# Scores and masks of unit 15 eight slots later in the fourth group's first step

## The chip, the cores and the metric

The kernel runs on one core of a Trainium2 chip. The core has a matrix engine (TensorE, PE in the profile; its weight loads stand apart as PEld), VectorE (DVE), ScalarE (ACT), GpSimd (POOL) and SyncE (SP), which issues most of the DMAs. The metric is the device time of one execution in microseconds, as the median of several runs.

## What is computed

Two stages follow each other: a linear attention with decay, block by block, and a bilinear feed-forward layer on its output.

```python
for b in range(nb):
    qb, kb, vb = (q[:, :, sl], k[:, :, sl], v[:, :, sl])
    intra = np.einsum('bhic,bhjc->bhij', qb, kb) * Dmask[None]
    intra = np.einsum('bhij,bhjd->bhid', intra, vb)
    inter = np.einsum('bhid,bhde->bhie', qb * lam_pow[None], kv_state)
    out[:, :, sl] = intra + inter
    kb_dec = kb * rev_pow[None]
    kv_state = lam_block * kv_state + np.einsum('bhsd,bhse->bhde', kb_dec, vb)
...
a = x @ w_a
b = x @ w_b
return a * b @ w_out
```

There are 4 batches, 8 heads, 768 positions and a head size of 64; x has 3072 rows of 512, and the hidden size is 1536.

## The kernel before

**Units and groups.** The 3072 rows are cut into 24 *units* of 128 positions (six for each batch), and the units into seven groups of 4, 2, 4, 4, 4, 4 and 2. While the feed-forward layer of one group runs, the attention of later units is fitted in between. The fourth group (group 3 in the code) holds units 10 to 13; during it the attention of units 14 to 17 is computed, which are the rows of the fifth group.

**What one unit's attention needs.** Its q and k are loaded by SP. POOL multiplies them by powers of the decay into one bf16 tile qk (line 276), then issues the load of v (line 298). SP transposes the tile by DMA into qkT (line 310). PE computes the unit's scores, eight matmuls into two banks of PSUM named kq (line 343, `scores`), and DVE multiplies each bank by a triangle of ones, giving two masked tiles m (line 360, `mask`). Together these last two are the piece "S" of the plan. Later a piece "O2" or "Q" adds up the outputs of two units from qkT, m, v and the running state. Piece "P" is POOL's scaling and all that hangs on it.

**The feed-forward layer of a full group** (`ffn_seven`) replaces eight block products by seven, with sums of blocks. Six *rounds* (0 to 5) cover the hidden size, two tiles of 128 at a time. Each round has seven products, called 1, 5, 2, 6, 3, 7 and 4 in the order in which they start, of four matmuls each (line 564), into accumulators m_q (1, 6, 7, 4), m_r (5, 3) and m_p (2). Between them ScalarE copies accumulators into SBUF (line 579) and DVE adds: c11 (line 598; in round 0 of this group on POOL, line 601), c12 (line 609), c22 (line 615), and the second half of the result ab (line 618). POOL makes the first half of ab (line 611) from c11 and c12. The tile of c12 has two buffers, so the c12 of one round waits for POOL's ab of two rounds before. The rounds overlap:

```python
for off, m in ((0, 1), (2, 5), (3, 2), (4, 6), (6, 3), (8, 7), (12, 4)):
    at[7 * i + off] = (i, m)
```

Then `out_seven` multiplies ab by the output weights in the same manner, beginning with o_q (line 675), which reads the POOL half of rounds 0, 2 and 4; DVE sums blocks of ab for it (lines 708 to 714) and the next group's rows (xs, lines 542 to 545).

**What sets the order.** Each engine runs its instructions in the order in which the program issues them. The table `PLAN` says for each group at which slot which piece is issued. In the rounds, slot 0 comes behind the first product of round 0, and slot 7 behind product 6 of round 3; slots 11 and later lie behind the rounds and in the output stage. At slot 17 of the group before, a piece "G" makes POOL wait for the sums xs of the next group, and the pieces "P" of units 15 and 16 stand behind it; those of units 17, 18 and 19 stand at slots 1, 4 and 7 of the fourth group. Seven banks of PSUM go round: a new accumulator takes the one that was longest out of use.

Of the kernel before, what the change touches and what calls it, by code (L numbers as in the profile page):

```python
# [22 lines left out]
def _bc(ap, dims):  # L23
# [33 lines left out]
        (6, "V", 8), (6, "P", 11), (7, "S", 9), (12, "O2", (8, 9))],  # L57
    2: [(0, "TO", 1), (0, "TO", 2), (0, "GT", None), (1, "P", 12), (4, "P", 13), (7, "P", 14), (10, "S", 10), (11, "S", 11),
        (17, "G", None), (17, "P", 15), (17, "P", 16)],
    3: [(0, "S", 15), (1, "P", 17), (4, "P", 18), (7, "P", 19), (17, "G", None), (17, "P", 20)],  # L60
    4: [(1, "P", 21), (4, "P", 22), (7, "P", 23)],
    5: [(11, "V", 22), (13, "O2", (22, 23))],
}
# [996 lines left out]
```

## Time and profile before

| what | us |
|---|---|
| median of 3 runs | 225.63 (225.57 to 226.48) |
| profiled execution | 225.45 |
| its span in the trace | 223.2 |
| PE busy | 211.4 (95%) |
| DVE busy | 175.2 (78%) |
| POOL busy | 126.5 (57%) |
| ACT busy | 109.4 (49%) |
| mean granted clock of PE | 0.985 of full speed |

The span runs from the first to the last instruction of the trace; the rest of the execution's time lies around it. A row of a timeline gives the start from the span's beginning, the length, the engine, the line, the operation with output and inputs, how many instructions were merged, and in brackets how long the engine stood idle before it and what ended that. A row of the windows gives the stretch, its length, then the busy time of PE, PEld, DVE, ACT and POOL with counts, the granted clock, the DMA share and the rate. The list of waits has the total, the number and the longest.

### The profile page before, as it was taken

The numbers are of one execution on the slowest core, as the hardware profiler recorded it, in microseconds if no ns is written. First come the engines' busy times: TensorE is split into PE (matmuls) and PEld (weight loads), VectorE is DVE, ScalarE is ACT, GpSimd is POOL, SyncE is SP. The second block draws the span as 40 slices with busy tenths as digits, with TensorE's granted clock in tenths as the row PEclk, the third lists the DMA queues.
The fourth block names the chain that finished last, engine by engine and source line by source line (L and its number), as shares of the span: only waits on it lengthen the run. The fifth ranks groups of instructions, "written<-read, shape, count | busy, mean of one in ns | idle before, by whom it ended". The sixth has DMA issues, their size and how long they took to land.

```text
span 223.2 us, 5802 instructions
## 1 busy us (share of the span) xinstructions
PE 211.4 (95%) x2339; PEld 163.8 (73%) x2347; DVE 175.2 (78%) x320; ACT 109.4 (49%) x199; POOL 126.5 (57%) x144
## 2 busy tenths in 40 slices
PE   7799999999999999999199999999999999999994
PEld 2476444557985888877078888788887888889973
DVE  0992999867888987999058899978899887996860
ACT  3586233358842755454055545275637366443522
POOL 5879659955676599505559940479930065310230
PEclk9999999999999999999679999999999999999999
DMA  4999999999799999991999993199950310001302
GB/s 132 291 181 187 202 228 213 226 222 155 147 162 167 142 151 217 266 149 51 188 245 150 181 152 54 49 194 176 105 49 3 139 52 0 3 0 54 138 3 94
DMA packets 84654, 30.78 MB, mean 138 GB/s; under 512 B 71956, under 2 KB 81044, under 8 KB 84628
## 3 DMA queue, kind: packets, MB, share of 16 engines
q1 hardware_dynamic: 51636, 19.86, 45.4%
q0 software_dynamic: 32704, 10.49, 41.6%
q8 instruction: 18, 0.29, 0.6%
q10 hardware_dynamic: 288, 0.07, 0.1%
q14 instruction: 8, 0.07, 0.1%
HBM read 28.32 MB, written 6.29 MB: 155 GB/s over the span
## 4 chain that ended last, share of the span: by engine, by line
PE 84%; issue 5%; DMA 5%; POOL 1%; SPq 1%; DVE 1%; ACT 0%; POOLq 0%
PE m_q L564 24%; PE m_r L564 12%; PE op L801 9%; PE o_q L675 7%; PE m_p L564 6%; PE b_ps L487 5%; PE a_ps L487 5%; PE o_ps L379 4%; PE o_r L675 4%; DMA k<-in_k_dram 3%; DMA qkT<-qk 2%; PE kq L343 2%; PE o_p L675 2%; SPq L229 1%; PE tps L321 1%
## 5 line engine op out<-in xcount | busy, mean ns | idle before, releaser
L564 PEld LDWEIGHTS <-tw 128*128 128x128 bf16 x576 | 49.3, 98 | 5.8 <-issue 0.2
L611 POOL TENSOR_TENSOR ab<-c,c 128x512 bf16<-128x512 bf16 x30 | 34.8, 1168 | 29.9 <-DVE c L609 29.6
L564 PE MATMUL m_q<-xs,tw 128*128 128x256 bf16 (+1 forms) x288 | 36.6, 257 | 0.0
L360 DVE TENSOR_TENSOR m<-kq,lotri 128x512 bf16<-128x512 f32 x47 | 29.5, 681 | 7.7 <-PE kq L343 7.7
L564 PEld LDWEIGHTS <-wa_sb 128*128 128x128 bf16 x288 | 25.0, 99 | 2.9
L579 ACT COPY s<-m_q 128x512 f32<-128x512 f32 x30 | 17.7, 590 | 16.8 <-PE m_q L564 15.7
L618 DVE TENSOR_TENSOR ab<-c,m_q 128x512 bf16<-128x512 f32 x30 | 20.6, 685 | 6.7 <-PE m_q L564 4.5
L609 DVE TENSOR_TENSOR c<-u,m_r 128x512 f32<-128x512 f32 x30 | 20.4, 681 | 5.2 <-ACT u L579 2.9
L579 ACT COPY s<-m_r 128x512 f32<-128x512 f32 x30 | 17.7, 590 | 13.3 <-PE m_r L564 13.3
L298 POOL DMA_DIRECT2D vb<-in_v_dram x24 | 22.3, 933 | 1.4 <-DMA wo_sb<-in_moe_w_out_dram 1.2
L801 PE MATMUL op<-wo_sb,ab 128*128 128x512 bf16 (+2 forms) x114 | 22.1, 335 | 0.4 <-issue 0.2
L601 POOL TENSOR_TENSOR c<-s 128x512 bf16<-128x512 f32 x7 | 9.1, 1295 | 21.3 <-ACT s L579 21.3
L615 DVE TENSOR_TENSOR c<-s,m_q 128x512 f32<-128x512 f32 x30 | 20.6, 686 | 0.6
L579 ACT COPY u<-m_q 128x512 f32<-128x512 f32 x30 | 17.8, 593 | 6.6 <-PE m_q L564 6.3
L675 PEld LDWEIGHTS <-sm 128*128 128x128 bf16 x192 | 17.5, 98 | 3.6 <-DVE sm L714 0.4
L598 DVE TENSOR_TENSOR c<-s,m_p 128x512 bf16<-128x512 f32 x23 | 15.8, 687 | 5.2 <-PE m_p L564 5.0
L276 POOL TENSOR_TENSOR qk<-qf,lp_q 128x512 bf16<-128x512 f32 x18 | 18.8, 1044 | 1.3 <-DMA qf<-in_q_dram 1.3
L564 PE MATMUL m_p<-xT,wa_sb 128*128 128x256 bf16 (+1 forms) x144 | 18.5, 259 | 0.0
L564 PE MATMUL m_r<-xs,tw 128*128 128x256 bf16 (+1 forms) x144 | 18.5, 259 | 0.0
L564 PE MATMUL m_r<-xs,wb_sb 128*128 128x256 bf16 (+1 forms) x144 | 18.4, 258 | 0.0
L402 ACT CAST xT<-o_ps 128x512 bf16<-128x512 f32 x22 | 11.9, 589 | 12.7 <-PE o_ps L379 12.4
L564 PE MATMUL m_q<-xT,tw 128*128 128x256 bf16 (+1 forms) x144 | 18.1, 255 | 0.0
(119 smaller groups left out, 376.0 us busy)
## 6 DMA issues: line engine op xcount, KB each, us to landing
out_dram<-o_two SPq DMA_DIRECT2D x8, 512.0 KB, 3.5
qf<-in_q_dram SPq DMA_DIRECT2D x14, 256.0 KB, 5.3
kf<-in_k_dram SPq DMA_DIRECT2D x14, 256.0 KB, 5.5
vb<-in_v_dram POOLq DMA_DIRECT2D x24, 128.0 KB, 5.5
wa_sb<-in_moe_w_a_dram POOLq DMA_DIRECT2D x6, 256.0 KB, 6.2
wb_sb<-in_moe_w_b_dram POOLq DMA_DIRECT2D x6, 256.0 KB, 7.7
wo_sb<-in_moe_w_out_dram POOLq DMA_DIRECT2D x6, 256.0 KB, 8.1
out_dram<-o_kept SPq DMA_DIRECT2D x6, 256.0 KB, 4.5
```

The source lines that it names most:

```text
L276: eng_of(eng).tensor_mul(dst.rearrange("p (c b) d -> p b c d", b=2), x[:].rearrange("p (b c) d -> p b c d", b=2), lp.rearrange("p (b c) o ...
L298: nc.gpsimd.dma_start(out=vb, in_=vr[b, nb])
L360: nc.vector.tensor_mul(m, kq[i], lotri_bc)
L487: nc.tensor.matmul(ps[:, lo:hi], lhsT=w_sb[:, s, f * 128:(f + 1) * 128], rhs=xT[:, s, lo:hi], start=(s == 0), stop=(s == KS - 1), skip_gro ...
L564: nc.tensor.matmul(ps[:, f, :], lhsT=w(k, f), rhs=x[:, k, :], start=(first and f == 0 and k == 0), stop=True, skip_group_check=True)
L579: nc.scalar.copy(t, ps)
L609: nc.vector.tensor_add(c12, d["u2"], d["r"])
L611: nc.gpsimd.tensor_mul(ab[:, nf * i:nf * i + nf, 0:h], d["c11"], c12)
L615: nc.vector.tensor_add(d["c22"], d["s5"], d["q"])
L618: nc.vector.tensor_mul(ab[:, nf * i:nf * i + nf, h:2 * h], d["c22"], d["q"])
L675: nc.tensor.matmul(ps[:, t, :], lhsT=x(j, c)[:, t * BLK:(t + 1) * BLK], rhs=w(j)[:, c, :], start=(first and t == 0 and j == js[0] and c == ...
L801: nc.tensor.matmul(op[:, lo:hi], lhsT=ab[:, f, t * 128:(t + 1) * 128], rhs=wo_sb[:, f, lo:hi], start=(f == 0), stop=(f == FC - 1))
```

## The change

One entry of the plan moves: the piece "S" of unit 15 goes from slot 0 of the fourth group to slot 7, ahead of the piece "P" of unit 19.

```diff
-    3: [(0, "S", 15), (1, "P", 17), (4, "P", 18), (7, "P", 19), (17, "G", None), (17, "P", 20)],
+    3: [(1, "P", 17), (4, "P", 18), (7, "S", 15), (7, "P", 19), (17, "G", None), (17, "P", 20)],
```

On PE, at the start of the fourth group, the program before has the last matmul of product 1 and then the scores of unit 15 (a row is a line of the code, the instruction and its operands with the tiles' numbers; in brackets stand the counters that it waits for, DMAHW being those of SP's DMAs):

```order
L564 LDWEIGHTS wa_sb_96
L564 MATMUL m_q_1957<-xT_1331,wa_sb_96 128x256
L343 LDWEIGHTS qkT_1908 [waits DMAHW1_49]
L343 MATMUL kq0_1964<-qkT_1908 128x128 [waits Activation_49]
L343 LDWEIGHTS qkT_1908
L343 MATMUL kq1_1965<-qkT_1908 128x128 [waits Activation_49]
```

With the change the same place reads so:

```order
L564 LDWEIGHTS wa_sb_96
L564 MATMUL m_q_1957<-xT_1331,wa_sb_96 128x256
L564 LDWEIGHTS tw_495
L564 MATMUL m_r_1964<-xs_1861,tw_495 128x256 [waits Activation_49]
L564 LDWEIGHTS tw_495
```

Product 5 of round 0 (m_r) now follows product 1 directly, and the weight load that waits for the transposing DMA is gone from here. On PE behind product 6 of round 3 (m_q_2104), the change has:

```order
L564 LDWEIGHTS tw_574
L564 MATMUL m_q_2104<-xs_1861,tw_574 128x256
L343 LDWEIGHTS qkT_1908 [waits DMAHW1_49]
L343 MATMUL kq0_2137<-qkT_1908 128x128 [waits DVE_49]
L343 LDWEIGHTS qkT_1908
L343 MATMUL kq1_2138<-qkT_1908 128x128 [waits DVE_49]
```

The wait for the DMA moves with the scores; behind the eight score matmuls comes product 4 of round 2. On DVE, at the group's start, the program before has the masks of unit 14, those of unit 15, and the first sums of round 0 and 1:

```order
L360 TENSOR_TENSOR m_1937<-kq_1927,lotri 128x512
L360 TENSOR_TENSOR m_1939<-kq_1928,lotri 128x512
L360 TENSOR_TENSOR m_1974<-kq_1964,lotri 128x512
L360 TENSOR_TENSOR m_1976<-kq_1965,lotri 128x512
L609 TENSOR_TENSOR c_2014<-u_1997,m_r 128x512
```

With the change the masks of unit 15 (m_2147 and m_2149) stand in rounds 2 and 3, behind c22 of round 2 and c11 of round 3:

```order
L615 TENSOR_TENSOR c_2115<-s_2077,m_q 128x512
L598 TENSOR_TENSOR c_2129<-s_2109,m_p 128x512
L360 TENSOR_TENSOR m_2147<-kq_2137,lotri 128x512
L360 TENSOR_TENSOR m_2149<-kq_2138,lotri 128x512
L618 TENSOR_TENSOR ab<-c_2115,m_q 128x2x256
L609 TENSOR_TENSOR c_2171<-u_2135,m_r 128x512
L615 TENSOR_TENSOR c_2185<-s_2122,m_q 128x512
```

So on DVE they come ahead of the second half of ab of round 2 and of c12 and c22 of round 3. ScalarE, POOL and SP have the same instructions in the same order as before.

## The prediction

> **What bounds the kernel now.** I read the page first, then the list of waits, then the chain that ended last around the longest wait, then the timeline and the windows of that stage. The page says which engine to watch:
>
> ```profile
> span 223.2 us, 5802 instructions
> ## 1 busy us (share of the span) xinstructions
> PE 211.4 (95%) x2339; PEld 163.8 (73%) x2347; DVE 175.2 (78%) x320; ACT 109.4 (49%) x199; POOL 126.5 (57%) x144
> ```
>
> TensorE (PE) is busy nearly all the time, so what is to be gained is where it stands still or runs slowly. In the list of waits, PE's longest is this one:
>
> ```profile
> PE kq L343 <- DMA qkT<-qk: 5.3, 1, 5.3
> ```
>
> It happens once. The timeline of PE puts it behind the first product of the fourth group (round 0, product 1), and the third row shows where that group's rounds end and its first output product begins:
>
> ```profile
> 105.08 0.60 PE L564 MATMUL m_q<-xT,wa_sb 128*128 128x256 bf16 x4
> 110.95 0.61 PE L343 MATMUL kq<-qkT 64*128 64x128 bf16 x8 [5.27 <-DMA qkT<-qk]
> ...
> 130.78 1.47 PE L675 MATMUL o_q<-wo_sb,ab 128*128 128x256 bf16 x12
> ```
>
> The chain that ended last shows what the eight score matmuls waited for, and what followed:
>
> ```profile
> 105.39 5.52 DMA qkT<-qk
> 110.91 0.04 issue
> 110.95 0.61 PE kq L343 x6
> 111.56 0.97 PE m_r L564 x4
> 112.53 0.85 PE m_p L564 x4
> 113.38 0.85 PE m_q L564 x4
> 114.23 0.77 PE m_r L564 x4
> 115.00 0.87 PE m_q L564 x8
> ```
>
> GpSimd (POOL) had only just scaled unit 15; its transposing DMA started at 105.39 and landed at 110.91. The four products after the wait are slow as well: 0.97, 0.85, 0.85 and 0.77 us where eight matmuls take 0.87, so 0.435 for four. That is 3.44 - 4 x 0.435 = 1.70 us of slow clock. The windows agree; the first is the fourth group's rounds, the second those of the fifth, which does the same products without scores among them, and the third lies just behind the wait (the column before the last two is the granted clock):
>
> ```profile
> 105.08:130.78 25.70, 20.43 (x178) 17.36 (x176) 15.32 (x24) 11.62 (x20) 19.80 (x20) 0.87 1.36 190
> 144.32:162.62 18.30, 18.30 (x170) 16.25 (x168) 15.06 (x24) 11.33 (x20) 16.72 (x17) 1.00 1.18 165
> 111.00:115.00 4.00, 4.00 (x26) 2.85 (x27) 1.29 (x2) 1.76 (x3) 0.91 (x1) 0.53 1.55 224
> ```
>
> So the fourth group's rounds take 7.40 us longer than the fifth's. 5.27 is the wait, 1.70 the slow clock, and the remaining 0.43 about what eight score matmuls take.
>
> **The change, part by part.** No instruction is added or removed. The unit's eight score matmuls go behind product 6 of round 3, their two masks on VectorE (DVE) before that round's next instruction, and the banks of PSUM are dealt out in another order within the group. POOL and SyncE (SP) keep their order, so no DMA is moved.
>
> *Removed at the old place.* Product 5 of round 0 follows product 1 at once. Had PE nothing else to wait for, the group would take 18.30 us as the fifth does, plus the scores. The scores have a price inside a group in the third one:
>
> ```profile
> 87.61 0.60 PE L564 MATMUL m_q<-xs,tw 128*128 128x256 bf16 x4
> 88.14 0.40 PE L343 MATMUL kq<-qkT 64*128 64x128 bf16 x8
> 88.47 0.61 PE L564 MATMUL m_r<-xs,tw 128*128 128x256 bf16 x4
> ```
>
> From 87.61 to 88.47 are 0.86 us, less 0.44 for the four matmuls of m_q: 0.42. PE alone would reach o_q at 105.08 + 18.30 + 0.42 = 123.80, a gain of 6.98. The scores themselves come at about 115.74 in the new place (product 4 of round 3, placed at 118.79 below, less the seven products of a round, 7 x 0.435), 4.8 us after the transposed tile has landed.
>
> *What POOL allows.* POOL does not wait for PE at the group's start; it is busy with unit 16:
>
> ```profile
> 108.26 0.94 POOL L298 DMA_DIRECT2D vb<-in_v_dram  x1
> 114.09 1.26 POOL L601 TENSOR_TENSOR c<-s 128x512 bf16<-128x512 f32 x1 [4.89 <-ACT s L579]
> ...
> 118.27 2.30 POOL L611 TENSOR_TENSOR ab<-c,c 128x512 bf16<-128x512 bf16 x2
> ...
> 124.60 1.04 POOL L276 TENSOR_TENSOR qk<-kf,lp_k 128x512 bf16<-128x512 f32 x1
> ...
> 127.54 2.29 POOL L611 TENSOR_TENSOR ab<-c,c 128x512 bf16<-128x512 bf16 x2
> 131.25 1.17 POOL L611 TENSOR_TENSOR ab<-c,c 128x512 bf16<-128x512 bf16 x1 [1.42 <-DVE c L609]
> ```
>
> Its sum c11 of round 0 now has its operands early, but POOL comes free only at 108.26 + 0.94 = 109.20 instead of 114.09. From there to 129.83 (the end of the ab product of round 4) it ran without a gap, so the whole row moves by 4.89 us and no more: the ab products of rounds 0 and 1 to 113.38, that of round 4 ends at 129.83 - 4.89 = 124.94. PE needs it for the fifth of the twelve matmuls of o_q, 0.44 after o_q begins. Before, that was 131.22, and POOL was done 1.39 ahead. Now PE would ask at 124.24 and POOL answers at 124.94: **POOL ends last**.
>
> *What DVE costs.* Two delays fall on DVE, both read against the fifth group, whose times I move by 144.32 - 105.08 = 39.24:
>
> ```profile
> 153.16 0.68 DVE L609 TENSOR_TENSOR c<-u,m_r 128x512 f32<-128x512 f32 x1
> ...
> 156.92 0.69 DVE L615 TENSOR_TENSOR c<-s,m_q 128x512 f32<-128x512 f32 x1
> ...
> 158.03 0.60 PE L564 MATMUL m_q<-xT,tw 128*128 128x256 bf16 x4
> ```
>
> The sum c12 of round 2 (153.16, so 113.92 here) writes a buffer, one of two, which the ab product of round 0 reads until about 113.38 + 1.15 = 114.53: it starts some 0.65 late. Queued behind it are c22 of round 2, c11 of round 3, the two masks, and then ab, c12 and c22 of round 3, each some 0.6 after the one ahead (the two masks before were busy 1.29 together, the only DVE work from 111 to 115). Counted from 114.6 that puts c22 of round 3 at 118.8, ending at 119.5. Product 4 of round 3 (158.03, so 118.79, plus 0.42 for the scores: 119.21) waits for it: about 0.35 us. DVE is busy 15.06 of 18.30 us in the fifth group, so it catches up. So PE reaches o_q at 123.80 + 0.35 = 124.15 and its fifth matmul at 124.59. That is still before POOL's 124.94, which with some 0.04 to pass the signal (110.91 to 110.95 at the old wait) makes 125.0.
>
> *Masks at the old place* cost nothing before, as DVE stood idle there, and their removal gives nothing. ScalarE's copies only follow PE. The first rounds now take their banks of PSUM from the same predecessors as those of the fifth group, where PE is busy 18.30 of 18.30 us; the scores take theirs from sums of rounds 1 and 2, which are done by then.
>
> *The new short wait and the clock.* By the rows a wait of 0.4 us costs between no slow clock and a share of what the long one cost, 1.70 x 0.4 / 5.27 = 0.13; I take none, the nearer of two ends that hardly differ. The Trainium skill (TensorE: Matmul & The Clock Gate, Part 1, What's actually happening) says that the clock halves only after an idle window of about 3.4 us. By that rule the short wait costs its own length alone and the sum stays at 6.2, by the share 6.1; the trace agrees for the long wait (0.53 behind it), and no quoted row tests a short one.
>
> *Sum.* The fifth matmul of o_q moves from 131.22 to 125.0: **6.2 us**. What follows in the group hangs on o_q, on POOL's last ab product and on DVE's sums, which keep their distances, and POOL's next preparation is gated by the next group's sums, so all later work should move as one. The profiled execution took 225.45 us, 2.25 outside its span: 225.45 - 6.2 = 219.25. The median of the runs is 0.18 above it, so I predict **219.4**.
>
> **The rivals.**
>
> *POOL's lateness is passed on whole.* POOL moves by 4.89 only, and the 1.39 of slack that I count as used may not be there for what follows o_q, where DVE sums the ab tiles:
>
> ```profile
> L708 DVE TENSOR_TENSOR sm<-ab x4: 414/416/1011, 93.7 to 131.7; 128x512 bf16<-128x512 bf16 x4
> ```
>
> The last, at 131.7, is the one of 1011 ns; it lay beside POOL's ab product of round 5 (131.25 to 132.42), and the median is 416. If these sums cannot pass POOL's ab product of round 5, a later one holds them back, and PE's next products behind them. Then the gain is POOL's 4.89 alone: 225.63 - 4.9 = 220.7. The Trainium skill (SBUF — State Buffer, SBUF: two separate sides) says that a DVE operation with two SBUF inputs and a POOL operation that reads SBUF lock each other out for a whole instruction; the long row agrees. Against this rival: by the times above the ab product of round 5 follows round 4's at 124.94, as near to o_q as before.
>
> *The slow clock is not the wait's* but returns in this group anyway: PE's path becomes 124.15 + 1.70 = 125.85, the gain 4.9, the time 220.7 too. Against it: the fifth group shows 1.00 throughout.
>
> *The wait only changes its name*, or the scores still wait at the new place: 225.6. Against it: the tile landed at 110.91, and product 5 reads the sums xs, on which POOL's work for unit 15 was itself gated, so they are older than the tile.
>
> *Slower: POOL comes too early for a load.* Unit 19 is now wanted at 124.60 - 4.89 = 119.71, and its load is issued no earlier than before:
>
> ```profile
> 112.02 1.40 SPq L151 DMA_DIRECT2D kf<-in_k_dram  x1
> DMA to landing us min/median/max: 5.3/5.7/6.6
> ```
>
> At 6.6 us it lands at 118.6, 1.1 ahead. Landing later than 119.71 stops POOL with three ab products behind it, and o_q with them. The gain is lost at 6.2 us of lateness, and with 1.70 of slow clock after so long a wait at 4.5. Above 5.6, a landing more than 13.3 us after the issue, the kernel is over 0.5% slower; at 7 it would be 225.63 - 6.2 + 7 + 1.7 = 228.1. No load of k in this stage took over 6.6 us.
>
> **How the numbers follow.** My forecast (gains of 5.6 to 7.0) gets 0.75, POOL passed on 0.11, the clock 0.06, the wait renamed 0.04, slower 0.04. The forecast's best end is 225.63 - 6.98 = 218.65, with 0.1 for the runs' spread 218.5; the high end takes in both cases at 220.7 with 0.5 for stalls that I count too small: 221.2. Both signs do not share the chance, so one range is enough. A measurement can tell 0.5% (1.1 us) from no change: faster 0.92, same 0.04, slower 0.04.
>
> **What would show it right or wrong.** PE's list should no longer hold the wait of kq for qkT, and the clock should be 1.00 from 105 to 125. c11 of round 0 on POOL should start near 109.2, with no gap to about 124.9. o_q should begin near 124.2 and wait about 0.4 for POOL's ab. Product 4 of round 3 should wait 0.3 or so for DVE. The fifth group should take 18.3 us again. A wait of POOL for kf, a low clock, or a wait of more than 1 us of PE in the group would prove a step wrong.

## The result and the profile after

The changed kernel took 219.14 us (median of 5 runs, 218.88 to 221.47) against 225.63 before (median of 5, 225.25 to 226.48). The means of the runs have a ratio of 0.9727 (95% interval 0.9674 to 0.978), so it is 2.7% faster. The forecast was 219.4. The piece S moved by seven slots, from slot 0 to slot 7, not by eight as the title has it. The profiled execution took 218.88 us. Its page, with the row of the granted clock:

```profile
span 216.8 us, 5801 instructions
## 1 busy us (share of the span) xinstructions
PE 209.9 (97%) x2339; PEld 162.7 (75%) x2347; DVE 175.0 (81%) x320; ACT 109.1 (50%) x199; POOL 126.5 (58%) x144
...
PEclk9999999999999999999999999999999999999999
```

PE is busy 1.5 us less for the same number of matmuls: the products that ran behind the wait at a low clock are gone, and the clock's row has nines throughout. The list of PE's waits, in full down to 0.3 us (the total, how often, the longest):

```profile
PE idle L213 <- DVE st L208: 1.3, 1, 1.3
PE tq L870 <- DVE scratch L863: 0.6, 2, 0.3
PE tk L870 <- DVE scratch L863: 0.5, 2, 0.3
PE o_q L675 <- POOL ab L611: 0.3, 1, 0.3
```

The 5.3 us of kq for qkT are not there any more. What is new is the last row, a short wait for POOL. PE's timeline shows where the scores stand now, and both places that cost something:

```profile
104.95 0.60 PE L564 MATMUL m_q<-xT,wa_sb 128*128 128x256 bf16 x4
105.39 0.60 PE L564 MATMUL m_r<-xs,tw 128*128 128x256 bf16 x4
...
115.70 0.40 PE L343 MATMUL kq<-qkT 64*128 64x128 bf16 x8
116.03 0.61 PE L564 MATMUL m_q<-xT,tw 128*128 128x256 bf16 x4
...
118.66 0.60 PE L564 MATMUL m_q<-xs,tw 128*128 128x256 bf16 x4
119.40 0.60 PE L564 MATMUL m_q<-xT,tw 128*128 128x256 bf16 x4
...
123.99 0.60 PE L675 MATMUL o_q<-wo_sb,ab 128*128 128x256 bf16 x4
124.90 1.05 PE L675 MATMUL o_q<-wo_sb,ab 128*128 128x256 bf16 x8 [0.32 <-POOL ab L611]
```

Product 5 follows product 1 at the pace of 0.44. From product 6 of round 4 to product 4 of round 3 (118.66 to 119.40) are 0.74 us instead of 0.44, a wait of 0.30. The list of waits does not hold it, because a row's length of 0.60 reaches past the next start, so that the profile sees only a gap of 0.14. From the first to the fifth matmul of o_q (123.99 to 124.90) are 0.91 instead of 0.44: starts are 0.47 late there, of which the profile books 0.32 as a wait. POOL's timeline has what that matmul waits for:

```profile
108.14 0.94 POOL L298 DMA_DIRECT2D vb<-in_v_dram  x1
109.09 1.28 POOL L601 TENSOR_TENSOR c<-s 128x512 bf16<-128x512 f32 x1
...
113.27 2.29 POOL L611 TENSOR_TENSOR ab<-c,c 128x512 bf16<-128x512 bf16 x2
...
122.54 3.42 POOL L611 TENSOR_TENSOR ab<-c,c 128x512 bf16<-128x512 bf16 x3
```

c11 starts the moment POOL is free (109.09). The three ab products of rounds 3 to 5 now run on end; two of the three take some 2.3 us, so the one of round 4 ends near 124.85, and o_q goes on at 124.90. DVE's timeline around the masks:

```profile
114.48 0.69 DVE L609 TENSOR_TENSOR c<-u,m_r 128x512 f32<-128x512 f32 x1 [0.60 <-PE m_q L564]
115.08 0.68 DVE L615 TENSOR_TENSOR c<-s,m_q 128x512 f32<-128x512 f32 x1
115.68 0.68 DVE L598 TENSOR_TENSOR c<-s,m_p 128x512 bf16<-128x512 f32 x1
116.28 1.28 DVE L360 TENSOR_TENSOR m<-kq,lotri 128x512 bf16<-128x512 f32 x2
117.48 0.67 DVE L618 TENSOR_TENSOR ab<-c,m_q 128x512 bf16<-128x512 f32 x1
118.07 0.68 DVE L609 TENSOR_TENSOR c<-u,m_r 128x512 f32<-128x512 f32 x1
118.67 0.68 DVE L615 TENSOR_TENSOR c<-s,m_q 128x512 f32<-128x512 f32 x1
```

c12 of round 2 stands idle for 0.60 us, then DVE works without a gap, and c22 of round 3 ends at 119.35, just ahead of product 4 at 119.40. The profile names PE as releaser of the idle time, but the sum's other condition ends later: POOL's ab of round 0, begun at 113.27, ends near 114.43. The first experiment shows that this is the one.

The windows close the account (fourth group's rounds, then the fifth's):

```profile
104.95:123.99 19.04, 18.90 (x179) 16.38 (x177) 14.84 (x24) 11.34 (x20) 18.96 (x20) 1.00 1.39 215
138.00:156.30 18.30, 18.30 (x170) 16.24 (x169) 15.05 (x24) 11.34 (x20) 16.75 (x17) 1.00 1.14 163
```

19.04 is the fifth group's 18.30, 0.42 for the scores, 0.30 for DVE. From the fourth group's first product to the fifth group's (138.01 in PE's timeline) are 33.06 us; before they were 144.32 - 105.08 = 39.24. The difference, **6.18 us, is the whole gain** but for 0.2 us of the span.

### The profile page after: what moved, and what is told of

Read it like the earlier page. It is cut to its first block, busy times and chain, and to the rows that moved or that the text cites. A ratio compares the mean times of both kernels' runs of the same rounds, so it can differ in the third digit from the quotient of the medians.

```text
span 216.8 us, 5801 instructions
## 1 busy us (share of the span) xinstructions
PE 209.9 (97%) x2339; PEld 162.7 (75%) x2347; DVE 175.0 (81%) x320; ACT 109.1 (50%) x199; POOL 126.5 (58%) x144
## 4 chain that ended last, share of the span: by engine, by line
PE 84%; POOL 7%; DMA 3%; SPq 1%; ACT 1%; DVE 1%; issue 1%
PE m_q L564 20%; PE m_r L564 10%; PE op L801 10%; PE o_q L675 9%; PE o_r L675 5%; PE o_ps L379 5%; PE m_p L564 5%; PE b_ps L487 5%; PE a_ps L487 5%; PE kq L343 3%; POOL qk L276 3%; DMA k<-in_k_dram 3%; POOL ab L611 3%; PE o_p L675 2%; PE kvd L410 1%; SPq L229 1%
## 5 line engine op out<-in xcount | busy, mean ns | idle before, releaser
L564 PE MATMUL m_q<-xs,tw 128*128 128x256 bf16 (+1 forms) x288 | 36.1, 255 | 0.0
L564 PE MATMUL m_q<-xT,wa_sb 128*128 128x256 bf16 (+1 forms) x144 | 18.1, 255 | 0.0
```

The costliest lines, as they stand in the source:

```text
L564: nc.tensor.matmul(ps[:, f, :], lhsT=w(k, f), rhs=x[:, k, :], start=(first and f == 0 and k == 0), stop=True, skip_group_check=True)
```

## The experiments

In the table the *group* is the time from the fourth group's first product to the fifth group's, from PE's timeline of the one profiled execution of each kernel. It leaves out the work ahead of it, which varies by over a microsecond from one profiled execution to another (the group's first product came between 104.9 and 106.2). The kernel before ran beside the experiments too: 225.66 with c12_three, pool_less, pool_more and slot3, and 225.34 with the other four. So a few tenths between totals of different sets decide nothing.

| kernel | us (median, range, runs) | group us | against the change |
|---|---|---|---|
| before | 225.63 (225.25 to 226.48, 5) | 39.24 | +6.18 |
| the change (slot 7) | 219.14 (218.88 to 221.47, 5) | 33.06 | |
| c12_three | 220.14 (1) | 33.05 | -0.01 |
| pool_less | 218.64 (218.28 to 218.96, 6) | 32.33 | -0.73 |
| pool_more | 220.03 (219.86 to 220.31, 4) | 34.36 | +1.30 |
| slot3 | 220.04 (219.35 to 221.29, 4) | 33.68 | +0.62 |
| slot2 | 220.95 (219.84 to 222.47, 4) | 34.31 | +1.25 |
| slot1 | 223.95 (223.07 to 226.34, 10) | 37.28 | +4.22 |
| slot8 | 219.07 (218.86 to 219.66, 4) | 33.07 | +0.01 |
| less_slot8 | 218.19 (218.03 to 218.24, 4) | 32.17 | -0.89 |

### Is it POOL that ends last, or DVE?

*c12_three: the wait of c12 for POOL taken away by a third buffer.*

```diff
-                c12 = sn_pool.tile([128, nf, h], F32, name="c12", tag="c12", bufs=2)
+                c12 = sn_pool.tile([128, nf, h], F32, name="c12", tag="c12", bufs=3)
...
-        s1 = snap("o_s1", "c12", q, 2)
+        s1 = snap("o_s1", "c12", q, 3)
...
-        u2 = snap("o_u2", "c12", q, 2)
+        u2 = snap("o_u2", "c12", q, 3)
...
-        o_sb = o_sb or o_pool.tile([128, d_model], F32, name="o_sb", tag="osb")
+        o_sb = o_sb or wst_pool.tile([128, d_model], F32, name="o_sb", tag="wst")
```

> The changed kernel with three buffers for c12 in place of two (and the last group's o_sb taken from another pool to make room), so that c12 of round 2 no longer waits for POOL's ab of round 0. Theory (two delays on DVE, of which the masks are the later; POOL ends last): c12 of round 2 starts near 113.8 instead of 114.48; product 4 of round 3 waits about 0.2 instead of 0.30 us, since the masks still cannot start before 116.1; PE then waits 0.4 instead of 0.32 at o_q and the fifth matmul of o_q stays at 124.9; the time stays at 219.1. Rival (the wait of product 4 comes from the c12 buffer alone): the wait is gone. Rival (POOL is not the last): o_q comes 0.3 earlier, 218.8.

This run's fourth group began at 106.20, 1.25 later than in the change's profile, so its times stand against that start. From DVE's and PE's timelines:

```profile
115.04 0.68 DVE L609 TENSOR_TENSOR c<-u,m_r 128x512 f32<-128x512 f32 x1
...
117.38 1.29 DVE L360 TENSOR_TENSOR m<-kq,lotri 128x512 bf16<-128x512 f32 x2
```

```profile
119.91 0.60 PE L564 MATMUL m_q<-xs,tw 128*128 128x256 bf16 x4
120.51 0.49 PE L564 MATMUL m_q<-xT,tw 128*128 128x256 bf16 x3
...
126.14 1.05 PE L675 MATMUL o_q<-wo_sb,ab 128*128 128x256 bf16 x8 [0.45 <-POOL ab L611]
```

c12 of round 2 comes 8.84 us into the group instead of 9.53, and DVE no longer stands idle before it, so it did wait for POOL's ab. The masks come at 11.18 instead of 11.33. They could not come sooner, as the scores ahead of them (116.95 to 117.35 in PE's timeline) had only just ended. Product 4 of round 3 starts at 120.51, 0.60 after product 6 of round 4: a wait of 0.16 instead of 0.30. PE gets to o_q 0.14 sooner and waits that much longer for POOL, 0.45 instead of 0.32; the group is as long as before. The total of 220.14, of a single run, missed the expected 219.1, and 1.25 us are lost ahead of the group. The third buffer is in use there too, but the loss is not its own: the run of slot1 below, which has two buffers, loses as much at the same two products of the second group (58.59 and 60.38 us here, 58.62 and 60.41 in slot1, 57.79 and 59.13 in the change). Within the group all of it went as the theory says: the masks and the buffer share the small wait, and POOL ends last.

*pool_less and pool_more: POOL's gapless row made shorter and longer by one sum.*

The table of the rounds whose c11 is summed on DVE changes in its entry for this group; first pool_less, then pool_more:

```diff
-3: (1, 2, 3, 4, 5)
+3: (0, 1, 2, 3, 4, 5)
```

> The changed kernel with the sum c11 of round 0 of the fourth group on DVE instead of POOL: POOL's gapless row is 1.25 us shorter. Theory (POOL ends last by 0.3, behind it DVE's masks by 0.3): ab of round 4 ends near 123.6 instead of 124.86, PE does not wait at o_q, c12 of round 2 does not wait for ab of round 0, product 4 of round 3 waits 0.2; the fifth matmul of o_q comes near 124.3 instead of 124.9, and the time falls by 0.6 to 218.5. Rival (POOL's lateness is hidden anyway): 219.1. Rival (DVE is the bound): slower, 219.7.

```diff
-3: (1, 2, 3, 4, 5)
+3: (2, 3, 4, 5)
```

> The changed kernel with the sum c11 of round 1 of the fourth group also on POOL instead of DVE: POOL's gapless row is 1.25 us longer. Theory (POOL ends last, and its lateness is passed on whole): ab of round 4 ends near 126.1, PE waits 1.6 us at o_q, the clock stays at 1.00 and the time rises by 1.25 to 220.4. Rival (POOL is not the bound): 219.1. Rival (any wait of PE above a microsecond brings slow clock): another 0.3 to 1.7 us, 220.7 to 222.1.

PE's timeline of pool_more at o_q:

```profile
123.92 0.60 PE L675 MATMUL o_q<-wo_sb,ab 128*128 128x256 bf16 x4
126.17 1.05 PE L675 MATMUL o_q<-wo_sb,ab 128*128 128x256 bf16 x8 [1.64 <-POOL ab L611]
```

A sum of 1.28 us more on POOL made the group 1.30 us longer, through this one wait of 1.64 (1.6 expected). So POOL's lateness is passed on whole from here. In the total 0.89 of it is seen (220.03, where 220.4 was expected); the span of the profiled execution is 1.3 longer, 218.1. One sum less took 0.73 off the group (0.6 expected); PE has no wait left at o_q, where its twelve matmuls run on end from 123.85. Of the 0.73, 0.47 is that wait; the rest comes from the rounds, which take 18.79 instead of 19.04. In the total 0.50 is seen, 218.64. Of the rest, 0.23 is given back in the fifth group, which takes 32.07 us from its first product to the sixth group's instead of 31.84; it is lost at product 3 of its first round. ScalarE's copy of product 5, which product 3 must wait for, starts 0.73 after the copy ahead of it there (138.07 to 138.80), and 0.48 in the change. Why it does so was not tried and stays open.

### The masks' place

*slot8: scores and masks one step later; less_slot8: with pool_less's edit as well.*

```diff
-    3: [(1, "P", 17), (4, "P", 18), (7, "S", 15), (7, "P", 19), (17, "G", None), (17, "P", 20)],
+    3: [(1, "P", 17), (4, "P", 18), (7, "P", 19), (8, "S", 15), (17, "G", None), (17, "P", 20)],
```

> Scores and masks of unit 15 at slot 8 of the fourth group, behind product 7 of round 3, where the masks come behind c22 of round 3 on DVE instead of ahead of it. Theory (POOL ends last): product 4 of round 3 no longer waits for DVE, nor does that of round 4; PE reaches o_q 0.3 earlier and waits 0.6 to 0.7 there instead of 0.32; the time stays at 219.1. Rival (the masks' place on DVE sets the end): 218.8. Rival (the masks delay the next rounds as much): a wait of 0.3 at product 4 of round 4 and 219.1 as well.

> Both together: c11 of round 0 of the fourth group on DVE, scores and masks of unit 15 at slot 8. Theory: neither wait is left in the fourth group's rounds, PE runs from 104.95 to o_q in 18.7 us, and the time is 0.75 below the changed kernel's, 218.4. Rival (something else in the output stage then ends last): as pool_less, 218.5, or 219.1.

With slot8 alone the group is the same, 33.07, as the theory says, but not by the way I expected. PE reaches o_q 18.96 us into the group, only 0.08 sooner instead of 0.3, and waits 0.41 there instead of 0.6 to 0.7. Product 4 of round 3 waits no more, but that of round 2 does, by 0.22, as PE's timeline of slot8 shows:

```profile
115.95 0.60 PE L564 MATMUL m_q<-xs,tw 128*128 128x256 bf16 x4
116.61 0.60 PE L564 MATMUL m_q<-xT,tw 128*128 128x256 bf16 x4
```

That is the late c12 of round 2, through c22. At slot 7 the eight score matmuls lie between and hide it. With both edits this delay is gone too; the windows of less_slot8 and a row of its POOL:

```profile
105.02:123.65 18.63, 18.63 (x178) 16.40 (x176) 15.66 (x25) 10.95 (x19) 18.34 (x19) 1.00 1.39 215
```

```profile
118.71 1.04 POOL L276 TENSOR_TENSOR qk<-kf,lp_k 128x512 bf16<-128x512 f32 x1 [0.21 <-DMA kf<-in_k_dram]
```

PE is busy 18.63 of 18.63 us. This is the best version found: 218.19 us, by the means 0.9679 of the kernel before (0.9662 to 0.9697), and 0.88 below slot8 on the same chip (218.03 to 218.24 against 218.86 to 219.66). The second row is the load of unit 19 that the prediction had as the way to a slower kernel: with POOL another 1.25 us earlier the load comes 0.21 too late. In pool_less POOL is as early and does not wait; SP issued the load at 112.10 there and at 112.75 here. So that margin was real, and about used up here.

### Waits of several lengths and the clock

*slot3, slot2 and slot1: the scores at places where the tile has not landed yet.*

```diff
-    3: [(1, "P", 17), (4, "P", 18), (7, "S", 15), (7, "P", 19), (17, "G", None), (17, "P", 20)],
+    3: [(1, "P", 17), (3, "S", 15), (4, "P", 18), (7, "P", 19), (17, "G", None), (17, "P", 20)],
```

> Scores and masks of unit 15 at slot 3 of the fourth group, behind product 6 of round 1. Theory: the scores come near 109.6 and wait about 1.2 us for the transposed tile that lands near 110.8; the clock stays at 1.00, as a wait shorter than about 3.4 us does not lower it; o_q's fifth matmul comes 0.7 later than with slot 7, the time is 219.9. Rival (slow clock in proportion to the wait): 0.4 more, 220.3. Rival (any wait costs the full slow clock of 1.7): 221.6.

In slot2 the entry is (2, "S", 15) at the same place of the list.

> Scores and masks of unit 15 at slot 2 of the fourth group, behind product 7 of round 0. Theory: the scores come near 108.3 and wait about 2.5 us for the transposed tile; no slow clock behind a wait shorter than about 3.4 us; the time is 2.0 above that of slot 7, 221.1. Rival (slow clock in proportion to the wait, 1.70 for 5.27): 0.8 more, 221.9. Rival (any wait costs the full 1.7): 222.8.

In slot1 it is (1, "S", 15), ahead of (1, "P", 17).

> Scores and masks of unit 15 at slot 1 of the fourth group, behind product 6 of round 0 and ahead of the piece P of unit 17. Theory: the scores come near 106.9 and wait about 3.9 us; that is near the length from which the clock falls, so either 222.5 with a clock of 1.00 or up to 224.2 with slow products behind the wait as at slot 0. Rival (slow clock in proportion): 223.7.

For each, PE's wait and the window of the 4 us behind it. First slot3, then slot2, then slot1:

```profile
111.26 0.40 PE L343 MATMUL kq<-qkT 64*128 64x128 bf16 x8 [1.17 <-DMA qkT<-qk]
```

```profile
111.30:115.30 4.00, 4.00 (x41) 3.36 (x42) 3.60 (x6) 1.61 (x3) 3.98 (x5) 1.00 1.56 221
```

```profile
110.37 0.40 PE L343 MATMUL kq<-qkT 64*128 64x128 bf16 x8 [1.96 <-DMA qkT<-qk]
```

```profile
110.40:114.40 4.00, 4.00 (x42) 3.53 (x43) 3.57 (x6) 1.76 (x3) 3.98 (x5) 1.00 1.56 212
```

```profile
111.64 0.41 PE L343 MATMUL kq<-qkT 64*128 64x128 bf16 x8 [3.48 <-DMA qkT<-qk]
111.98 1.04 PE L564 MATMUL m_r<-xs,wb_sb 128*128 128x256 bf16 x4
...
115.34 0.60 PE L564 MATMUL m_p<-xT,wa_sb 128*128 128x256 bf16 x4
```

```profile
111.60:115.60 4.00, 3.96 (x27) 2.87 (x28) 2.57 (x4) 0.59 (x1) 3.98 (x5) 0.57 1.53 206
```

In these traces, waits of 1.17 and 1.96 us leave the clock at 1.00; behind a wait of 3.48 it is 0.57, and four products then take 3.36 us (111.98 to 115.34) instead of 1.75, a loss of 1.61. Behind the 5.27 us of the kernel before, four products take 3.35 from start to start (111.49 to 114.84 in PE's timeline), a loss of 1.60; the prediction's 1.70 adds up the chain's rows instead. There the eight scores were slow as well, 0.54 us where the change has 0.33. So the loss is about 1.8 against 1.6, and hardly grows with the wait between these two. Both rivals of slot3 and slot2, a share of the wait and the full 1.7 behind any wait, fall for the executions profiled. Where the clock falls and returns is read from windows of 1 us, at first in the kernel before, then in slot1:

```profile
107.00:108.00 1.00, 0.00 (x0) 0.00 (x0) 0.00 (x0) 0.00 (x0) 1.00 (x2) 0.98 0.86 116
...
114.00:115.00 1.00, 1.00 (x8) 0.75 (x6) 0.00 (x0) 0.59 (x2) 0.91 (x1) 0.60 1.29 272
```

```profile
111.00:112.00 1.00, 0.36 (x9) 0.25 (x10) 0.00 (x0) 0.00 (x0) 1.00 (x2) 0.95 1.29 202
...
115.00:116.00 1.00, 1.00 (x9) 0.83 (x8) 0.44 (x1) 0.40 (x1) 0.73 (x1) 0.84 1.29 239
```

Between the two rows of each the clock is 0.50. A mean of 0.98 is then 0.04 us of slow clock in that window, and so on: the clock is low from 107.96 to 114.80 in the kernel before, 6.84 us, and from 111.90 to 115.32 in slot1, 3.42 us or half as long. In the kernel before it fell about 2.3 us after PE's last matmul had ended (105.08 + 0.60), in slot1 0.26 after PE had begun again (111.64). So the length of the wait alone does not tell whether the clock falls, and a wait of some 2 us is not shown to be safe: the slowest of slot2's four runs, 222.47 us, has a mean clock of 0.992, which 3.5 us at 0.50 would give. It has no trace, so where its clock was low stays open. The Trainium skill (TensorE: Matmul & The Clock Gate, Part 1, What's actually happening) says that the clock halves after at least one idle window of about 3.4 us, and that this window runs freely. The stretches of 3.42 and 6.84 us agree with such a window, but the fall after 2.3 us without a matmul does not agree with a window that has to be wholly idle.

The sizes: slot3's group is 0.62 longer (0.7 expected), slot2's 1.25 (2.0 expected), since its tile landed sooner and the wait was 1.96 instead of 2.5 us, and since PE does not wait the 0.30 at product 4 of round 3 that it waits in the change; its four runs spread from 219.84 to 222.47 about the expected 221.1. slot1 came out at 223.95, near the upper end of 222.5 to 224.2.

## Why the prediction was right

**The wait and its slow clock (6.98 us removed).** Both are gone. slot1 and the kernel before have them at another length each, and the traces of slot2 and slot3 have the wait without the slow clock, so the two parts are shown apart.

**POOL moves by 4.89 only and ends last.** POOL was predicted to start c11 at 109.20 and to be done with round 4's ab at 124.94; it did at 109.09 and near 124.85. pool_more shows that each microsecond of POOL is then one of the kernel, pool_less and c12_three that PE was waiting for POOL and nothing else there. The cost was 0.47 us, for 0.41 predicted (125.0 against 124.59).

**DVE costs 0.35 at product 4 of round 3.** Measured 0.30. The chain of seven instructions behind the late c12 was counted to end at 119.5 and ended at 119.35. That this wait does not show in the end, as POOL is later still, is shown by c12_three's one run: it halved, and the group stayed.

**The sum.** 6.2 predicted, 6.18 measured from group to group. The remaining 0.26 us between 219.4 and 219.14 lies outside the group and was not predicted: between the two profiled executions 0.13 is ahead of it (its first product at 104.95 instead of 105.08), some 0.1 behind it and 0.17 outside the span.

**The rivals.** *POOL's lateness passed on whole* asked for a gain of 4.89; the slack of 1.39 was there. DVE's first sum of the ab tiles did stretch beside POOL's last ab product (of 410, 416 and 1290 ns the longest), yet the output stage, from o_q to the fifth group, took 14.02 - 0.47 = 13.55 us, as before (144.32 - 130.78 = 13.54). *The slow clock* did not return (1.00 in the group's rounds). *The renamed wait* did not come: product 5 ran at once. *The late load* had its margin, and lost it only in less_slot8.

**The clock's rule.** The sum took no slow clock for the short wait, and that held: PE's wait at o_q was 0.47 and the clock's row shows nines. The idle window cited there is not borne out as a limit for the wait, as the clock of the kernel before fell after some 2.3 us; nothing in the sum hangs on it.

## What to carry to other kernels

A wait on a DMA is best taken away by putting other work of the same engine ahead of it, and its price is the wait and, where the clock fell, a piece of slow clock behind it (some 1.6 and 1.8 us in the two traces that have it). Which waits are too short for that is not settled by these runs. What comes back is less than both, because engines that did not wait stay where they were: follow the row of each of them (here POOL's) from the moment when it was really free, and see by how much its last result precedes its reader. An instruction that is moved into a busy stage is paid for on every engine of its chain; look for a step where other work already hides what it delays.

## What the runs showed of the hardware

The slow clock behind a long wait cost nearly the same for 3.48 and for 5.27 us (some 1.6 and 1.8), although the clock was low for 3.42 us in one and for 6.84 in the other: in the kernel before, the first 3 us of the low stretch lay in the wait itself (107.96 to 110.95). In the kernel before the clock fell when PE had stood still for only some 2.3 us. I had not expected that the work ahead of the fourth group differs by 1.25 us between profiled executions, as in c12_three and slot1, while the group itself comes out within 0.02 us in three kernels that should take the same (33.05, 33.06 and 33.07).
